# Two feed-forward layers behind a gated linear attention: a new list scheduler for the engine orders, a later place for the second weights' narrowing, and a graded lead in the last block

## The chip, the cores and the metric

The kernel runs on one core of a Trainium2 chip (trn2). The metric is the device time of one execution in microseconds; less is better.

## What is computed

```python
def _attn_ref(q, k, v, f_logit):          # q, k, v, f_logit: (4, 8, 768, 48)
    f = 1.0 / (1.0 + np.exp(-f_logit))
    for t in range(S):
        state = f[:, :, t, :, None] * state + np.einsum('bhd,bhe->bhde', k[:, :, t], v[:, :, t])
        y[:, :, t] = np.einsum('bhd,bhde->bhe', q[:, :, t], state)

def _moe_ref(x, w_in, w_out):             # x: (3072, 384), w_in: (384, 2048), w_out: (2048, 384)
    h = x @ w_in
    return (h * np.clip(h + 3.0, 0.0, 6.0) / 6.0) @ w_out

def _moe2_ref(x, w_in, w_out):            # same shapes
    h = x @ w_in
    return (h * np.tanh(np.log1p(np.exp(h)))) @ w_out

attn_out = _attn_ref(...)                 # transposed to (3072, 384)
out = _moe2_ref(_moe_ref(attn_out, ...), ...)
```

## The kernel before

The 3072 tokens go through in six blocks of 512, twice: once through the first layer (phase 1) and once through the second (phase 2). A layer has 16 parts of 128 hidden columns. For one part of one block TensorE makes a hidden run `H` of nine 128x512 matmuls (line 497; three chunks of the model dimension, each as high-by-high, low-by-high and high-by-low halves of an fp32r split), VectorE and ScalarE turn the result `h` into `g` and split it into `gh` and `gl` (lines 513 to 532: in phase 1 ScalarE's relu, VectorE's clip and product on L517, ScalarE's copy to `gh`, VectorE's subtraction to `gl` on L203), and TensorE adds three output runs `O` of three matmuls each into the banks o0 to o2 (line 538). Six blocks, two layers and 16 parts make 192 such rounds of 18 matmuls.

Phase 1 takes its input from the attention (line 236), which is worked out in 24 units of 128 tokens, four to a block. A unit has a running sum of the logs (`tri` times `f`, or a scan on VectorE, L278), a transposition of `k`, the scores `a`, masks, and the values; the state `st` goes from unit to unit. From the ninth unit on (`SPLIT`) a unit works in two halves of 64 tokens, its `v` is loaded with the line 258 and ScalarE copies the state into it.

The weights come in 64 bits. For one part, a load brings 768 KB into one of two tiles `raw` (line 211), and two ScalarE and two VectorE instructions narrow it into a tile `we` (lines 218 to 223, VectorE's on L220 and L222). For the first layer `weight` splits it at once into `wh` and `wl` (line 226). For the second layer, it is written to memory (`w2_d`, line 607) and read again at the start of phase 2.

Nothing of this is issued in the order it is written. `Plan.op` (line 89) records each step with its engine, a cost in microseconds, what it reads and writes, and a rank; `Plan.emit` (line 114) then runs one list schedule forward: on each engine the ready step of the lowest rank comes next. Ranks are written by hand: `16 * j + f` for a part, due times for the attention's units, `W2_AT + W2_GAP * f` for the second layer's narrowing, and in the last block all of the last `HOLD` = 14 parts lead by `TAIL_LEAD` = 6. Where TensorE would be idle before the first layer begins, `emit` puts in filler matmuls that write an unused bank (`warm`, `o<-cap` in the profile), one unit of 128 columns for each 0.22 us of planned idle time. All loads and stores are issued by SyncE's queue (SP), in the planned order.

```python
            now, eng = min((max(free[e], min(o.ready for o in c)), e) for e, c in wait.items() if c)
            o = min((o for o in wait[eng] if o.ready <= now), key=lambda o: (o.rank, o.seq))
            ...
                if free[eng] and free[eng] + unit < now < limit:
                    order.append(int((now - free[eng]) / unit))
```

Of the kernel before, what the change touches and what calls it, by code (L numbers as in the profile page):

```python
# [9 lines left out]
U32 = mybir.dt.uint32  # L10
# [6 lines left out]
DM, DFF, NT = 384, 2048, 3072  # L17
# [6 lines left out]
NF = DFF // 128  # L24
# [17 lines left out]
FIRST = "f0 tri k0 q0 f1 f2 ident v0 k1 q1 f3 v1 w0 k2 q2 v2 k3 q3 w1 v3 w2".split()  # L42
WARM = 30
GAP = 0.28
HOLD, TAIL_LEAD = 14, 6
WE = 2
W2_AT = 40
W2_GAP = 3.5
SPANS = ((0, D), (HB, R))


# [20 lines left out]


class Op:
    __slots__ = ("eng", "cost", "lat", "rank", "fn", "deps", "after", "seq", "start", "end", "left", "outs", "ready")


class Plan:
# [10 lines left out]
    def op(self, eng, cost, rank, fn, r=(), w=(), lat=0.0):  # L89
        o = Op()  # L90
        o.eng, o.cost, o.lat, o.rank, o.fn, o.seq = eng, cost, lat, rank, fn, len(self.ops)
        o.deps, o.after = set(), set()
        for key in r:
            o.deps.add(self.wrote[key])
        for key in w:
            o.deps.update(self.read.get(key, ()))
            if key in self.wrote:
                o.deps.add(self.wrote[key])
        for key in r:
            self.read.setdefault(key, []).append(o)  # L100
        for key in w:
            self.wrote[key], self.read[key] = o, []
        for key in (*r, *w):
            z = key[0] if isinstance(key, tuple) else key
            if isinstance(z, Lazy):
                z.users.append(o)
                if key in r:
                    z.used = True
                if not z.used:
                    z.heads.append(o)  # L110
        o.deps.discard(o)
        self.ops.append(o)

    def emit(self, filled, limit, unit, warm):
        for zs in self.tags.values():
            for i, z in enumerate(zs):
                if i:
                    for o in z.users:
                        o.after.update(zs[i - 1].heads)
                if i >= z.bufs:  # L120
                    for o in z.users:
                        o.deps.update(zs[i - z.bufs].users)
        for o in self.ops:
            o.outs, o.left, o.ready = [], 0, 0.0
        for o in self.ops:
            o.deps.discard(o)
            o.after -= o.deps | {o}
            for d in o.deps | o.after:
                d.outs.append(o)
            o.left = len(o.deps) + len(o.after)  # L130
        wait = {o.eng: [] for o in self.ops}
        free = dict.fromkeys(wait, 0.0)
        for o in self.ops:
            if not o.left:
                wait[o.eng].append(o)
        order = []
        while any(wait.values()):
            now, eng = min((max(free[e], min(o.ready for o in c)), e) for e, c in wait.items() if c)
            o = min((o for o in wait[eng] if o.ready <= now), key=lambda o: (o.rank, o.seq))
            wait[eng].remove(o)  # L140
            if eng == filled:
                limit = min(limit, now) if o.rank >= 1 else limit
                if free[eng] and free[eng] + unit < now < limit:
                    order.append(int((now - free[eng]) / unit))
            o.start, o.end = now, now + o.cost
            free[eng] = o.end
            order.append(o)
            for d in o.outs:
                t = o.start if d in o.after or o in d.after and o not in d.deps else \
                    o.end + o.lat + (GAP if d.eng != eng else 0.0)  # L150
                d.ready = max(d.ready, t)
                d.left -= 1
                if not d.left:
                    wait[d.eng].append(d)
        for o in order:
            if isinstance(o, int):
                warm(o)
            else:
                o.fn()


def fast_path(ctx, tc, qt, kt, ft, fn, vn, vs, vk, w1, w2, cst, ident, flag, w2_d, out):
    nc = tc.nc
    wide = w1.dtype != F32
# [27 lines left out]
    def dma(rank, out, in_, r, w, size, name=None):  # L192
        P.op("sp", max(0.45, size / 280e3), FIRST.index(name) - 99 if name in FIRST else rank, lambda: nc.sync.dma_start(out=out(), in_=in_()), r, w,
             lat=1.9)

    def pe(cost, rank, fn, r, w):
        P.op("pe", cost, rank, fn, r, w)
# [8 lines left out]
        dve(n, rank, lambda: nc.vector.tensor_tensor(out=out(), in0=a(), in1=b(), op=ALU.mult), r, w)  # L206


    def stream(w, f, rank, name=None):
        raw = new("raw", [128, 2 * DM * (2 if wide else 1)], 2, U32)  # L210
        dma(rank - 3, raw, lambda: w[f].bitcast(U32), (), (raw,), 128 * 2 * DM * (8 if wide else 4), name)
        if not wide:
            return raw, lambda: raw().bitcast(F32)
        e = new("we", [128, 2 * DM], WE)
        v = lambda i: raw().rearrange("p (a b) -> p a b", b=2)[:, :, i]
        eu = lambda: e().bitcast(U32)
        stt = nc.vector.scalar_tensor_tensor
# [271 lines left out]
    def hidden(ph, j, f, i):  # L489
        t0, n = BLOCKS[ph - 1][j]  # L490
        tail = ph == 2 and t0 + n == NT and f >= NF - HOLD
        xs = X[ph, j]
        tag, bufs = ("h", 2) if ph == 1 else (("h", 2), ("a", 2), ("m", 1), ("h", 2), ("a", 2))[i % 5]
        z = bank(tag, [128, 512], bufs)
# [7 lines left out]
                       stop=(t == 3 * KC - 1))  # L502
                    t += 1

        pe(9 * (0.0135 + n / 2400), i - TAIL_LEAD * tail, run, [("w", f, 0), ("w", f, 1), *x_keys(ph, j, 0), *x_keys(ph, j, 1)], (z,))
        if tail and f == NF - 1:
            gs = [new("A", [128, 2 * 512], 2, F32R) for p in "hl"]
        else:
# [3 lines left out]
        rank = i + 0.5  # L512
# [6 lines left out]
        else:  # L519
            e, g = new("k", [128, 512], 3), new("q", [128, 512], 3)  # L520
# [14 lines left out]
        for m in range(KC):  # L535
# [58 lines left out]
    for j, (t0, n) in enumerate(BLOCKS[0]):  # L594
# [3 lines left out]
        elif late:  # L598
            rank, values, vr, zxs, finish = late.pop()
# [3 lines left out]
        for f in range(NF):  # L603
            hidden(1, j, f, 16 * j + f)
    for f in range(NF):
        key, src = stream(w2, f, W2_AT + W2_GAP * f)
        dma(W2_AT + 1 + W2_GAP * f, lambda f=f: w2_d[f], src, (key,), (("w2", f),), 128 * DM * 8)

    def check1():
# [9 lines left out]
    for j, (t0, n) in enumerate(BLOCKS[1]):  # L619
# [17 lines left out]
        if j == 0:  # L637
            for f in range(NF):
                z = new("raw", [128, 2 * DM], 2)
# [196 lines left out]
```

## Time and profile before

| what | value |
|---|---|
| median of 3 runs | 894.73 us (893.9 to 894.84) |
| the profiled execution: its own time | 895.67 us |
| the profiled execution: its span | 893.9 us |
| TensorE (PE) busy in the span | 881.0 us, 99% |
| VectorE (DVE) busy | 668.7 us, 75% |
| ScalarE (ACT) busy | 561.5 us, 63% |
| loads and stores by SyncE's queue | 82.20 MB, 28.9% of 16 engines' span |

The profiled execution's own time is 1.77 us over its span and 0.94 us over the median. A timeline row gives the start in us, the duration in us, engine, line, operation, what it writes and reads, and in brackets how long the engine was idle before it and what ended that. Matmuls overlap, so a row's duration is longer than the step from one matmul to the next. PEld is TensorE's weight load.

### The profile page before, as it was taken

The page shows a single profiled execution, that of the slowest core. Times are in us where ns is not written, and L with a number is a line of the kernel's source. Part 1 is how long each engine was busy: PE and PEld are TensorE (multiplying, and loading weights), DVE is VectorE, ACT ScalarE, POOL GpSimd, SP SyncE. Part 2 cuts the span into 40 slices and gives each one's busy share as a digit, 9 for nine tenths or more (in the row PEclk, how much of TensorE's full clock was granted, in tenths as well). Part 3 has the DMA queues.
Part 4 walks back from the last instruction along what each step waited for, and adds up shares of the span by engine and source line. Part 5 has one row for each costly group of instructions (what it writes and reads, how often), then busy time and mean ns, then how long its engine had stood idle before and what let it go on. Part 6 is the DMA issues. An engine that isn't in the chain of part 4 may idle for free.

```text
span 893.9 us, 15680 instructions
## 1 busy us (share of the span) xinstructions
PE 881.0 (99%) x6341; PEld 722.0 (81%) x6341; DVE 668.7 (75%) x1045; ACT 561.5 (63%) x978; POOL 0.2 (0%) x4
## 2 busy tenths in 40 slices
PE   9999989999999999999999999999999999999997
PEld 6878868888888888888888888888888888888785
DVE  4898999778777555653565977888878888785894
ACT  6898787667646454433545766666666667664773
POOL 0000000000000000000000000000000000000000
PEclk9999999999999999999999999999999999999999
DMA  8766656867544222100323200100100100000001
GB/s 267 237 200 225 205 192 210 267 209 234 192 133 130 65 65 76 60 25 1 120 92 102 76 1 12 59 1 24 48 0 24 48 1 18 30 1 1 36 1 40
DMA packets 32465, 83.29 MB, mean 93 GB/s; under 512 B 3712, under 2 KB 7040, under 8 KB 32384
## 3 DMA queue, kind: packets, MB, share of 16 engines
q1 hardware_dynamic: 32384, 82.20, 28.9%
q8 instruction: 52, 0.85, 0.4%
q14 instruction: 29, 0.24, 0.1%
HBM read 66.45 MB, written 15.73 MB: 92 GB/s over the span
## 4 chain that ended last, share of the span: by engine, by line
PE 93%; ACT 2%; DVE 2%; DMA 1%; issue 0%; ACTq 0%
PE o L200 45%; PE h L200 30%; PE a L200 12%; PE m L200 7%; DMA raw<-w 1%; PE m L300 1%; ACT we L187 1%; ACT wh L187 0%; DVE we L220 0%; ACT raw L187 0%; DVE b L278 0%; DVE A L290 0%; PE m L400 0%; DVE we L222 0%; ACT vk L187 0%
## 5 line engine op out<-in xcount | busy, mean ns | idle before, releaser
L200 PE MATMUL o<-gh,wh 128*128 128x512 f32 x570 | 225.1, 395 | 0.0
L200 PE MATMUL o<-gl,wh 128*128 128x512 f32 x570 | 222.3, 390 | 0.7 <-DVE gl L203 0.7
L200 PE MATMUL o<-gh,wl 128*128 128x512 f32 x570 | 222.0, 389 | 0.0
L200 PE MATMUL h<-xh,wh 128*128 128x512 f32 x402 | 159.0, 396 | 2.1 <-DVE g L517 2.1
L200 PE MATMUL h<-xh,wl 128*128 128x512 f32 x402 | 157.3, 391 | 0.3 <-DVE wl L203 0.3
L200 PE MATMUL h<-xl,wh 128*128 128x512 f32 x402 | 157.0, 391 | 0.0
L200 PEld LDWEIGHTS o<-gh,wh 128*128 128x128 f32 x570 | 107.0, 188 | 24.2 <-issue 0.4
L200 PEld LDWEIGHTS o<-gh,wl 128*128 128x128 f32 x570 | 107.0, 188 | 22.6
L200 PEld LDWEIGHTS o<-gl,wh 128*128 128x128 f32 x570 | 107.1, 188 | 22.5 <-DVE gl L203 1.1
L517 DVE SCALAR_TENSOR_TENSOR g<-g,h 128x512 f32<-128x512 f32 x96 | 65.6, 684 | 79.1 <-ACT g L187 79.0
L187 ACT ACTIVATE g<-h,small 128x512 f32<-128x512 f32 x96 | 65.8, 686 | 82.3 <-PE h L200 69.7
L187 ACT ACTIVATE gh<-q 128x512 fp32r<-128x512 f32 x94 | 59.3, 631 | 79.8 <-DVE q L206 75.0
L203 DVE TENSOR_TENSOR gl<-g,gh 128x512 fp32r<-128x512 f32 x96 | 66.1, 689 | 33.4 <-ACT gh L187 33.1
L200 PEld LDWEIGHTS h<-xh,wh 128*128 128x128 f32 x402 | 75.6, 188 | 18.7 <-DVE g L517 2.7
L200 PEld LDWEIGHTS h<-xh,wl 128*128 128x128 f32 x402 | 75.7, 188 | 17.1 <-DVE wl L203 1.0
L200 PEld LDWEIGHTS h<-xl,wh 128*128 128x128 f32 x402 | 75.8, 188 | 15.2
L187 ACT ACTIVATE q<-k,small 128x512 f32<-128x512 f32 x96 | 69.4, 723 | 28.8 <-DVE k L525 25.1
L206 DVE TENSOR_TENSOR q<-q,k 128x512 f32<-128x512 f32 x96 | 66.0, 688 | 24.9 <-ACT q L187 23.5
L187 ACT ACTIVATE gh<-g 128x512 fp32r<-128x512 f32 x96 | 60.2, 627 | 35.3 <-DVE g L517 35.2
L203 DVE TENSOR_TENSOR gl<-q,gh 128x512 fp32r<-128x512 f32 x94 | 64.7, 688 | 9.2 <-ACT gh L187 8.5
L187 ACT ACTIVATE k<-k 128x512 f32<-128x512 f32 x96 | 59.6, 625 | 17.6 <-DVE k L522 17.4
L525 DVE SCALAR_TENSOR_TENSOR k<-k 128x512 f32<-128x512 f32 x96 | 65.3, 684 | 0.7 <-ACT k L187 0.7
(140 smaller groups left out, 1164.8 us busy)
## 6 DMA issues: line engine op xcount, KB each, us to landing
raw<-w SPq DMA_DIRECT2D x32, 768.0 KB, 5.2
v<-vs SPq DMA_DIRECT2D x16, 512.0 KB, 3.8
w<-we SPq DMA_DIRECT2D x16, 384.0 KB, 2.7
raw<-w SPq DMA_DIRECT2D x16, 384.0 KB, 3.0
k<-kt SPq DMA_DIRECT2D x24, 224.0 KB, 4.3
q<-qt SPq DMA_DIRECT2D x24, 224.0 KB, 3.6
x<-o SPq DMA_DIRECT2D x18, 256.0 KB, 2.1
f<-x SPq DMA_DIRECT2D x18, 256.0 KB, 2.6
```

Source lines behind the costliest of these rows:

```text
L187: lambda: nc.scalar.activation(out=out(), in_=in_(), func=func, **k), r, w)
L200: nc.tensor.matmul(**k)
L203: dve(n, rank, lambda: nc.vector.tensor_tensor(out=out(), in0=a(), in1=b().bitcast(F32), op=ALU.subtract), r, w)
L206: dve(n, rank, lambda: nc.vector.tensor_tensor(out=out(), in0=a(), in1=b(), op=ALU.mult), r, w)
L300: nc.tensor.transpose(ztv()[:, p, :], k3()[:, p, :], ident[0:R, 0:R])
L517: dve(n, rank, lambda: nc.vector.scalar_tensor_tensor(out=gg(), in0=gg(), scalar=6.0, in1=zn(), op0=ALU.min, op1=ALU.mult), (g, z), (g,))
L525: dve(n, rank, lambda: nc.vector.scalar_tensor_tensor(out=ee(), in0=ee(), scalar=2.0, in1=ee(), op0=ALU.add, op1=ALU.mult), (e,), (e,))
```

## The change

`emit` now makes seven forward list schedules (`ROUNDS` = 6, and the last) with a backward one between them. The first forward pass uses the ranks written by hand. A backward pass schedules every step as late as it can go, from the end of the pass before, and the time it gives a step is the step's rank in the next forward pass. Of the seven orders the one with the shortest planned end is issued. Since ranks are overwritten, `mlp` keeps which steps belonged to the layers.

The filler counts a unit double, 0.44 us, where planned idle time begins before `COLD` = 8 us. The load of part `f` of the second weights may start only when the hidden run number `22 + 3.5 f` of phase 1 is done (the new key `("h", i)`); its rank by hand is as before. In the last block the lead of a part grows in equal steps from 6/14 to 6.

```diff
+COLD = 8.0
+ROUNDS = 6
+W2_FROM = 22
...
+        o.mlp = rank >= 1
...
+    def forward(self):
+        wait = {o.eng: [] for o in self.ops}
+        free = dict.fromkeys(wait, 0.0)
+        for o in self.ops:
+            o.ready, o.left = 0.0, len(o.deps) + len(o.after)
...
+        while any(wait.values()):
+            now, eng = min((max(free[e], min(o.ready for o in c)), e) for e, c in wait.items() if c)
+            o = min((o for o in wait[eng] if o.ready <= now), key=lambda o: (o.rank, o.seq))
...
+        return max(o.end for o in self.ops)
+
+    def backward(self):
+        end = max(o.end for o in self.ops)
...
+        while any(wait.values()):
+            now, eng = max((min(free[e], max(o.ready for o in c)), e) for e, c in wait.items() if c)
+            o = max((o for o in wait[eng] if o.ready >= now), key=lambda o: (o.end, o.seq))
+            wait[eng].remove(o)
+            o.rank = now - o.cost
+            free[eng] = o.rank
+            for d in o.deps | o.after:
+                d.ready = min(d.ready, o.rank - d.lat - (GAP if d.eng != eng else 0.0) if d in o.deps else o.rank + d.cost)
...
     def emit(self, filled, limit, unit, warm):
...
+        best = None
+        for i in range(ROUNDS + 1):
+            end = self.forward()
+            if best is None or end < best[0]:
+                best = end, [(o, o.start, o.end) for o in self.ops]
+            if i < ROUNDS:
+                self.backward()
+        for o, o.start, o.end in best[1]:
+            pass
+        order, free = [], {}
+        for o in sorted(self.ops, key=lambda o: (o.start, o.seq)):
+            if o.eng == filled:
+                limit = min(limit, o.start) if o.mlp else limit
+                if o.eng in free:
+                    slow = unit * (2 if free[o.eng] < COLD else 1)
+                    if free[o.eng] + slow < o.start < limit:
+                        order.append(int((o.start - free[o.eng]) / slow))
+                free[o.eng] = o.end
             order.append(o)
...
-    def stream(w, f, rank, name=None):
+    def stream(w, f, rank, name=None, after=()):
         raw = new("raw", [128, 2 * DM * (2 if wide else 1)], 2, U32)
-        dma(rank - 3, raw, lambda: w[f].bitcast(U32), (), (raw,), 128 * 2 * DM * (8 if wide else 4), name)
+        dma(rank - 3, raw, lambda: w[f].bitcast(U32), after, (raw,), 128 * 2 * DM * (8 if wide else 4), name)
...
-        pe(9 * (0.0135 + n / 2400), i - TAIL_LEAD * tail, run, [("w", f, 0), ("w", f, 1), *x_keys(ph, j, 0), *x_keys(ph, j, 1)], (z,))
+        pe(9 * (0.0135 + n / 2400), i - (TAIL_LEAD * (f - NF + HOLD + 1) / HOLD if tail else 0), run, [("w", f, 0), ("w", f, 1), *x_keys(ph, j, 0), *x_keys(ph, j, 1)], (z, ("h", i)))
...
-        key, src = stream(w2, f, W2_AT + W2_GAP * f)
+        key, src = stream(w2, f, W2_AT + W2_GAP * f, after=(("h", int(W2_FROM + W2_GAP * f)),))
```

The orders change on every engine. Three places are shown; line numbers after the change are 40 higher in these parts.

TensorE at the start of the program, before: `cap` is the filler, `tri` the running sum of the first unit's logs, `ident` its transposition of `k`.

```order
L200 MATMUL o_147<-cap 112x128
L200 MATMUL o_147<-cap 112x512 x3
L200 MATMUL o_147<-cap 112x128 x2
L200 MATMUL o_164<-tri,f 112x128 x4
L200 MATMUL o_147<-cap 112x512 x2
L200 MATMUL o_147<-cap 112x128 x2
L400 MATMUL m<-ident,k 128x112 x4
```

And after the change:

```order
L240 MATMUL o_147<-cap 112x128
L240 MATMUL o_147<-cap 112x512
L240 MATMUL o_147<-cap 112x128 x3
L240 MATMUL o_164<-tri,f 112x128 x4
L240 MATMUL o_147<-cap 112x512
L240 MATMUL o_147<-cap 112x128
L440 MATMUL m<-ident,k 128x112 x4
```

The filler ahead of the first sum shrinks from 1 + 14 units of 128 columns to 1 + 7, and the one behind it from 10 to 5.

VectorE where the first block's parts end and the ninth and tenth units begin, before: `b<-cap,f` are the scans, `A<-q,b` and `A<-a,tri` the split units' work, `g` and `gl` the layer's, `we` the second weights' narrowing.

```order
L206 TENSOR_TENSOR k<-k,f 112x512
L290 TENSOR_TENSOR A<-q,b 64x512
L290 TENSOR_TENSOR A<-q,b 48x512
L203 TENSOR_TENSOR gl<-g,gh 128x512
L206 TENSOR_TENSOR k<-k,f 112x512
L290 TENSOR_TENSOR A<-q,b 64x512
L290 TENSOR_TENSOR A<-q,b 48x512
L220 SCALAR_TENSOR_TENSOR we<-we,raw 128x768
L329 TENSOR_TENSOR st<-st,a 112x192
L339 TENSOR_TENSOR A<-a,tri 64x256 x4
L517 SCALAR_TENSOR_TENSOR g<-g,h 128x512
```

And after the change:

```order
L246 TENSOR_TENSOR k<-k,f 112x512
L243 TENSOR_TENSOR gl<-g,gh 128x512
L330 TENSOR_TENSOR A<-q,b 64x512
L330 TENSOR_TENSOR A<-q,b 48x512
L246 TENSOR_TENSOR k<-k,f 112x512
L557 SCALAR_TENSOR_TENSOR g<-g,h 128x512
L330 TENSOR_TENSOR A<-q,b 64x512
L330 TENSOR_TENSOR A<-q,b 48x512
L243 TENSOR_TENSOR gl<-g,gh 128x512
L369 TENSOR_TENSOR st<-st,a 112x192
L379 TENSOR_TENSOR A<-a,tri 64x256 x4
L557 SCALAR_TENSOR_TENSOR g<-g,h 128x512
```

The layer's `gl` and `g` have moved ahead of the split units' work, and no narrowing stands here any more. In the order before, a whole pair of narrowing instructions (L220 and L222) also stands just ahead of this piece, and the L222 that belongs to the L220 shown follows a few rows behind it.

SyncE's queue where the third block's attention output `x` is stored, before:

```order
L193 DMA f<-ft 112x512 x2
L193 DMA x_2_130<-o 128x512 x3
L193 DMA v<-vs 128x1024
L193 DMA vk<-vk 128x384
L193 DMA k<-kt 112x512
L193 DMA q<-qt 112x512
L193 DMA v<-vs 128x1024
```

And after the change, a little further on:

```order
L233 DMA x_2_130<-o 128x512
L233 DMA raw<-w 128x1536
L233 DMA q<-qt 112x512
L233 DMA w_8_70<-we 128x768
L233 DMA raw<-w 128x1536
L233 DMA v<-vs 128x1024
L233 DMA vk<-vk 128x384
L233 DMA k<-kt 112x512
L233 DMA q<-qt 112x512
```

A 768 KB load of the second weights now stands right ahead of a unit's `v`, 512 KB. That is so for 5 of the 16 loads of `v<-vs`; before it was so for 3.

## Rows read from the trace of the kernel before

**Rows 1.** The page's part 1: busy time, share of the span, instructions.

```profile
PE 881.0 (99%) x6341; PEld 722.0 (81%) x6341; DVE 668.7 (75%) x1045; ACT 561.5 (63%) x978; POOL 0.2 (0%) x4
```

**Rows 2.** Waits of PE: us in total, times, longest us.

```profile
PE h L200 <- DVE g L517: 2.1, 2, 1.9
...
PE m L200 <- DVE q L206: 1.3, 1, 1.3
PE o L200 <- DVE gl L203: 0.7, 1, 0.7
```

**Rows 3.** Windows: length, busy us of PE, PEld, DVE, ACT, POOL, PEclk, DMA share, GB/s.

```profile
4.00:8.00 4.00, 4.00 (x11) 1.83 (x10) 0.00 (x0) 0.58 (x1) 0.00 (x0) 1.00 1.05 324
8.00:33.00 25.00, 25.00 (x413) 20.77 (x412) 18.65 (x32) 20.59 (x47) 0.00 (x0) 1.00 0.83 255
33.00:113.00 80.00, 79.11 (x669) 63.87 (x667) 72.92 (x100) 67.69 (x114) 0.00 (x0) 1.00 0.67 218
...
123.70:127.10 3.40, 3.40 (x46) 2.36 (x47) 3.40 (x5) 3.36 (x8) 0.00 (x0) 0.52 0.06 23
...
887.70:893.90 6.20, 0.00 (x0) 0.00 (x0) 0.04 (x1) 0.60 (x1) 0.00 (x0) 0.81 0.39 137
```

**Rows 4.** Timeline of all engines, start of the program.

```profile
1.59 6.41 PE L200 MATMUL o<-cap 112*112 112x128 f32 x12 [1.59 <-DVE small L573]
...
4.03 0.58 ACT L187 ACTIVATE f<-f 128x448 f32<-128x448 f32 x1
...
7.84 1.04 PE L200 MATMUL o<-tri,f 128*112 128x128 f32 x8
8.71 2.32 PE L200 MATMUL o<-cap 112*112 112x512 f32 x8
```

**Rows 5.** Timeline of PE around the first hidden runs.

```profile
32.00 1.24 PE L200 MATMUL o<-cap 112*112 112x512 f32 x4
33.00 0.48 PE L200 MATMUL h<-xh,wh 128*128 128x512 f32 x1
...
35.15 0.55 PE L400 MATMUL m<-ident,k 112*128 112x112 f32 x4
...
36.72 0.50 PE L200 MATMUL h<-xh,wh 128*128 128x512 f32 x1
...
39.00 0.54 PE L200 MATMUL m<-v,kn 128*32 128x48 f32 x32
...
41.01 0.50 PE L200 MATMUL h<-xh,wh 128*128 128x512 f32 x1
...
43.32 0.39 PE L200 MATMUL o<-gh,wh 128*128 128x512 f32 x1
```

**Rows 6.** Timeline of DVE from the last input to the first part's `gl`.

```profile
32.16 0.55 DVE L203 TENSOR_TENSOR xl<-h,xh 128x384 fp32r<-128x384 f32 x1
...
38.62 0.68 DVE L517 SCALAR_TENSOR_TENSOR g<-g,h 128x512 f32<-128x512 f32 x1
...
42.35 0.69 DVE L203 TENSOR_TENSOR gl<-g,gh 128x512 fp32r<-128x512 f32 x1
```

**Rows 7.** Timeline of ACT in the same stretch.

```profile
38.82 1.00 ACT L187 ACTIVATE we<-raw 128x768 f32<-128x768 f32 x1 [1.18 <-DMA raw<-w]
```

**Rows 8.** Timeline of DVE, 109 to 122 us.

```profile
109.63 0.96 DVE L220 SCALAR_TENSOR_TENSOR we<-we,raw 128x768 uint32<-128x768 uint32 x1 [0.55 <-ACT raw L187]
...
118.96 0.96 DVE L220 SCALAR_TENSOR_TENSOR we<-we,raw 128x768 uint32<-128x768 uint32 x1
...
121.98 0.69 DVE L517 SCALAR_TENSOR_TENSOR g<-g,h 128x512 f32<-128x512 f32 x1
```

**Rows 9.** Timeline of PE at the longest wait.

```profile
122.72 0.50 PE L200 MATMUL h<-xh,wh 128*128 128x512 f32 x1 [1.86 <-DVE g L517]
```

**Rows 10.** The same, in the last block.

```profile
836.18 0.50 PE L200 MATMUL m<-xh,wh 128*128 128x512 f32 x1 [1.35 <-DVE q L206]
```

**Rows 11.** Waits of ACT, as in rows 2.

```profile
ACT v L187 <- DMA v<-vs: 19.0, 7, 2.9
```

More of the change, by code (lines that the diff above doesn't have):

```diff
@@ L74 @@
 class Op:
-    __slots__ = ("eng", "cost", "lat", "rank", "fn", "deps", "after", "seq", "start", "end", "left", "outs", "ready")
+    __slots__ = ("mlp", "eng", "cost", "lat", "rank", "fn", "deps", "after", "seq", "start", "end", "left", "outs", "ready")
 class Plan:
@@ L112, in op @@
         self.ops.append(o)
+    def forward(self):
[3 more added lines that the diff above has]
+            o.ready, o.left = 0.0, len(o.deps) + len(o.after)
+            if not o.left:
+                wait[o.eng].append(o)
+        while any(wait.values()):
+            now, eng = min((max(free[e], min(o.ready for o in c)), e) for e, c in wait.items() if c)
+            o = min((o for o in wait[eng] if o.ready <= now), key=lambda o: (o.rank, o.seq))
+            wait[eng].remove(o)
+            o.start, o.end = now, now + o.cost
+            free[eng] = o.end
+            for d in o.outs:
+                d.ready = max(d.ready, o.end + o.lat + (GAP if d.eng != eng else 0.0) if o in d.deps else o.start)
+                d.left -= 1
+                if not d.left:
+                    wait[d.eng].append(d)
+        return max(o.end for o in self.ops)
+    def backward(self):
+        end = max(o.end for o in self.ops)
+        wait = {o.eng: [] for o in self.ops}
+        free = dict.fromkeys(wait, end)
+        for o in self.ops:
+            o.ready, o.left = end, len(o.outs)
+            if not o.left:
+                wait[o.eng].append(o)
+        while any(wait.values()):
+            now, eng = max((min(free[e], max(o.ready for o in c)), e) for e, c in wait.items() if c)
+            o = max((o for o in wait[eng] if o.ready >= now), key=lambda o: (o.end, o.seq))
+            wait[eng].remove(o)
+            o.rank = now - o.cost
+            free[eng] = o.rank
+            for d in o.deps | o.after:
+                d.ready = min(d.ready, o.rank - d.lat - (GAP if d.eng != eng else 0.0) if d in o.deps else o.rank + d.cost)
+                d.left -= 1
+                if not d.left:
+                    wait[d.eng].append(d)
     def emit(self, filled, limit, unit, warm):
@@ L123, in emit @@
         for o in self.ops:
-            o.outs, o.left, o.ready = [], 0, 0.0
-        for o in self.ops:
             o.deps.discard(o)
             o.after -= o.deps | {o}
+            o.outs = []
+        for o in self.ops:
             for d in o.deps | o.after:
                 d.outs.append(o)
[L130 to L146, printed above, removed]
-            order.append(o)
[L148 to L154, printed above, removed]
+        best = None
[16 more added lines that the diff above has]
+                free[o.eng] = o.end
+            order.append(o)
         for o in order:
```

## The prediction

> **What bounds the kernel now.** First the busy shares [rows 1]: TensorE (PE) works through 99% of the span, VectorE through 75%, so the reader is to see that PE's stream of matmuls sets the time and that a new order can win only what that stream loses. The change alters no matmul of the computation. Three kinds of loss are to be looked for: idle time, filler, and time at half rate.
>
> The waits of PE [rows 2] give the idle time: 2.1 us for `g`, 1.3 for `q`, 0.7 for `gl`. The windows [rows 3] give the rest. From 8 to 33 us PE is busy throughout, but with filler and attention: the first hidden run starts at 33.00 [rows 5]. From 123.7 to 127.1 its granted clock is 0.52, which is the lower of its two levels (1.2 and 2.4 GHz) for nearly the whole of 3.40 us; just before, it had waited 1.86 us [rows 9]. The last 6.20 us hold no matmul at all; they are the last eviction and stores, which the change leaves alone.
>
> All but one of these losses lie where VectorE is crowded: it is busy for 72.92 of 80 us from 33 to 113 [rows 3]. The one in the last block, 1.35 us at 836.18 [rows 10], is of the order alone: hidden runs pulled forward all at once leave too few output runs to cover a part's chain.
>
> PE's idle time in the span is 893.9 - 881.0 = 12.9 us, of which 6.2 are the end. Beside this stands a rule of the Trainium skill (Perfetto Trace Analysis, section Identifying the Most-Contended Engine): matmul busy share is not a good measure of how close TensorE is to its limit, the share of weight loads is one of two better ones. By busy share alone at most 6.7 us could be won and the time would be no less than 888.0; the filler and the half-rate stretch, both counted as busy, say with the rule that there is more.
>
> **The change part by part.** The sum is made against the profiled execution's own 895.67 us, 0.94 over the median of the runs.
>
> *A, filler counted double before 8 us.* PE works off 15 units of filler from 1.59 to 8.00, 0.43 us each; behind the first sum 10 units take 2.32 us, 0.23 each [rows 4]. So the early ones run at half rate, though the recorded clock says 1.00 there [rows 3]. The logs that the first sum waits for are ready at 4.03 + 0.58 = 4.61, but PE is at filler until 8.00. With 8 units it is free at 1.59 + 8 x 0.43 = 5.0. If the sum then runs at half rate, it takes 2.1 instead of 1.04 us and ends at 7.1 instead of 8.9: 1.8 us earlier. The attention's chain hangs on it up to the first hidden run, whose last input ends at 32.71 [rows 6]. Bounds: 0, if the loads set the pace (the queue moves 324 GB/s from 4 to 8 us, [rows 3]); 3.0, if the sum runs at full rate. I take 1.8, since the loads in the first 12 us are issued in nearly the same order and none of them is awaited on this chain after the first.
>
> *B, attention work moved ahead of the first hidden run.* The fifth unit's transposition and scores stand between the first two hidden runs, from 35.15 to 36.72 [rows 5]; the new order puts them in front, where filler runs for 1.24 us and PE waits anyway. Gain 1.5; bounds 0 (if they push the hidden run back) and 1.6.
>
> *C, the first output run comes too early.* Before, 8.0 us lie between the end of the first hidden run (35.3) and its output run (43.32), filled with transposition, scores, a hidden run, values and another hidden run [rows 5]. Now only one hidden run and the values are left between: 39.00 - 36.72 + 41.01 - 39.00 = 4.3 us. The chain through ACT and VectorE took 7.7, to 42.35 + 0.69 [rows 6], 1.2 of it for a late load of weights [rows 7]. The new order leaves relu, `g`, a pair of narrowing instructions and `gl`: 0.68 (taken like `g`) + 0.68 + 2 x 0.96 + 0.69, with the hand-overs some 4.3 us, if nothing else holds them up. So a new wait of 0 to 3.7 us; I take 1.2, nearer to the lower end, because masks and scans that stood in this chain have gone ahead.
>
> *D, the second weights' narrowing leaves the crowded stretch.* Before, a pair of it starts at 109.63 and another at 118.96 [rows 8], in front of the `g` at 121.98 that PE waits for; each instruction is 0.96 us. Now the first load waits for hidden run 22, in the second block, and the layer's `gl` and `g` go ahead of the split units' work. I count the waits for `g` and `gl` as gone, 2.1 + 0.7, and with them the half-rate stretch, (1 - 0.52) x 3.40 = 1.6. What is late next is the split units' own masks, which other hidden and output runs cover. Bounds 0 and 4.4. The narrowing itself, 32 VectorE and 32 ACT instructions in all, half of them the second layer's, now lies beside PE work from the second block on, where VectorE has room.
>
> *E, stepwise lead in the last block.* Hidden runs and output runs now alternate; 1.3 us of waiting goes [rows 2, 10]. Bounds 0 and 1.3. The end behind the last matmul costs nothing and gains nothing.
>
> *F, the wait added on SyncE's queue.* A load of second weights that waits for its hidden run holds back all that is behind it, above all a unit's `v`. I cost it at 0: ACT already waits 19.0 us in 7 places for `v` [rows 11], up to 2.9 each, and no wait of PE for it is on the list of rows 2. Without that cover see the second rival.
>
> Sum: -1.8 - 1.5 + 1.2 - 4.4 - 1.3 = **-7.8 us**, 887.9 in a profiled execution, 886.9 in the median.
>
> **The rivals.**
>
> *The crowd comes back.* The orders are the best by planned costs; where PE runs behind plan, VectorE may be as full as before and half of D and E return, C at 2.7. For it: VectorE's share of 91% from 33 to 113 [rows 3] falls only where the narrowing leaves, the last ten us of it. Against: the `g` rows are really ahead now. Gain 1.8 + 1.5 - 2.7 + 2.8 = 3.4: 891.3.
>
> *ACT stands behind a late `v`.* Five `v` loads are queued right behind a 768 KB load. At 324 GB/s [rows 3] that takes 2.4 us, and ACT, which issues in order, keeps the layer's relu back for as long. If PE has used up its cover, as the waits of up to 2.9 us [rows 11] allow, that is 5 x 2.4 = 12 us: 886.9 + 12 = 898.9, slower than before. It decides from the point where such a wait of ACT is longer than the output runs that PE has ready; against it, the planner places its other steps with this order of loads in view, and the 2.9 us waits cost PE nothing.
>
> *The lower clock lasts.* Less filler means more idle time in the first 30 us; if the lower level then lasts to the first hidden run, A turns round. From 8 to 33 us ACT is busy 20.59 of 25.00 us [rows 3], so at least 4.4 us hang on PE's or the loads' steps alone, which double: -7.8 + 1.8 + 4.4 = -1.6, 893.1. For it: the level fell once, behind a wait of 1.86 us. Against: from 8 to 113 us the windows keep 1.00 [rows 3]. The Trainium skill (TensorE: Matmul & The Clock Gate, What's actually happening) says that the throttled state is the default and activity releases it, which speaks for this rival; rows 9 and 3 agree in the order of events, no more.
>
> *Nothing gained.* If the best order by plan is none on the chip, waits only move: 894.7.
>
> **How the numbers follow.** A measurement of this kernel can tell some 0.2%, 1.8 us, from no change. The forecast has 0.77, the crowd 0.11, the late `v` 0.06, the lower clock and nothing gained 0.03 each. All the best ends, 3.0 + 1.6 + 4.4 + 1.3 with no new wait, make 10.3: 884.4. On the other side the range takes in the crowd's 891.3; the bounds of A and C alone, 0 and 3.7, make the sum -3.5, 891.2. So 884.2 to 891.5; left out are the late `v`, the lower clock and no gain. Faster: 0.77 + 0.11 = 0.88; within 0.2%: 0.06 (lower clock and no gain); slower: 0.06.
>
> **What would show it.** Right: the first sum starts near 5 us and the first hidden run near 31; a new wait of about 1 us for `gl` before the first output run; no wait of PE over 0.5 us between 100 and 130 and none near 830; granted clock 1.00 from 100 to 140; no narrowing instruction between 100 and 140. Wrong: PE waits at the split units between 150 and 400 us (the late `v`), matmul steps at double length after 10 us (the lower clock), or new waits for `g` before 110 (the crowd).

## The result and the profile after

| | median us | lowest to highest | runs |
|---|---|---|---|
| before | 893.9 | 893.36 to 894.84 | 5 |
| changed | 884.42 | 883.22 to 886.42 | 5 |

The ratio is 0.9896, 95% interval 0.9882 to 0.991: 9.5 us faster, where 7.8 were forecast (884.42 against 886.9, range 884.2 to 891.5). The profiled execution of the changed kernel took 883.22 us, the shortest of its five, with a span of 881.5. Against the profile before (895.67) that is 12.4 us, 2.9 more than the medians differ by. The pair of profiles overstates the gain; a half-rate stretch and late loads, each of them in some executions of a kernel and not in others, account for part of that below.

The changed kernel's busy times (the page's part 1), to be read against [rows 1]:

```profile
PE 872.5 (99%) x6327; PEld 719.2 (82%) x6327; DVE 668.6 (76%) x1045; ACT 564.1 (64%) x978; POOL 0.2 (0%) x4
```

The share of PE is the same 99%, though 12 us of span are gone: PE's busy time itself fell by 8.5 us while its computation stayed as it was. The 14 instructions fewer are filler (40 of them before, 26 now); the rest is half-rate time and the ends of matmuls that overlap less around a wait.

All waits of PE in the changed kernel (us in total, times, longest):

```profile
PE o L240 <- DVE small L613: 1.6, 1, 1.6
PE o L240 <- DVE gl L243: 1.1, 1, 1.1
PE m L440 <- DVE k L246: 0.5, 1, 0.5
```

The first is the program's start, which is in every version. Of [rows 2] nothing is left: the waits for `g` and `q` are gone, the one for `gl` is another, at 37.84, ahead of the first output run. The windows of the changed kernel (columns as in [rows 3]):

```profile
8.00:33.00 25.00, 24.95 (x421) 21.50 (x420) 21.49 (x37) 22.70 (x50) 0.00 (x0) 1.00 0.89 291
33.00:113.00 80.00, 78.94 (x717) 64.12 (x716) 74.77 (x103) 68.14 (x117) 0.00 (x0) 1.00 0.59 194
100.00:120.00 20.00, 20.00 (x244) 16.40 (x246) 18.19 (x29) 16.59 (x37) 0.00 (x0) 1.00 0.27 82
120.00:140.00 20.00, 20.00 (x249) 16.50 (x239) 13.29 (x24) 12.89 (x27) 0.00 (x0) 1.00 0.34 111
820.00:840.00 20.00, 20.00 (x90) 16.57 (x89) 17.19 (x28) 13.55 (x22) 0.00 (x0) 1.00 0.02 9
```

From 100 to 140 PE never stops and keeps its full clock, where before it was at 0.52 from 123.7 to 127.1. No narrowing stands there: the last of it ends at 100.66 and the next begins at 151.62. VectorE is busier from 33 to 113 than in [rows 3], 74.77 against 72.92 us, and PE's idle time there is 1.06 us, all of it at one wait, against 80 - 79.11 = 0.89 before. So how full VectorE is does not by itself set PE's waits.

PE's start in the changed kernel (timeline), the answer to [rows 4, 5]:

```profile
1.59 3.69 PE L240 MATMUL o<-cap 112*112 112x128 f32 x10 [1.59 <-DVE small L613]
5.12 1.04 PE L240 MATMUL o<-tri,f 128*112 128x128 f32 x8
...
30.00 0.48 PE L240 MATMUL h<-xh,wh 128*128 128x512 f32 x1
...
32.15 0.39 PE L240 MATMUL h<-xh,wh 128*128 128x512 f32 x1
...
36.28 0.49 PE L240 MATMUL o<-gh,wh 128*128 128x512 f32 x1
37.84 0.50 PE L240 MATMUL o<-gl,wh 128*128 128x512 f32 x1 [1.06 <-DVE gl L243]
```

Three pieces make up the 12.4 us between the two profiles. The first hidden run starts at 30.00 instead of 33.00: 3.0. From there to the end of the last matmul it takes 875.67 - 30.00 = 845.7 us instead of 887.68 - 33.00 = 854.7: 9.0. The stores behind the last matmul take 5.8 instead of 6.2: 0.4. These two marks, the first hidden run and the length from it to the last matmul, are used for every run below.

### The profile page after: what moved, and what is told of

It reads as the page before. It is cut to its first block, busy times and chain, and to the rows that moved or that the text cites. A ratio compares the mean times of both kernels' runs of the same rounds, so it can differ in the third digit from the quotient of the medians.

```text
span 881.5 us, 15666 instructions
## 1 busy us (share of the span) xinstructions
PE 872.5 (99%) x6327; PEld 719.2 (82%) x6327; DVE 668.6 (76%) x1045; ACT 564.1 (64%) x978; POOL 0.2 (0%) x4
## 4 chain that ended last, share of the span: by engine, by line
PE 97%; DVE 1%; ACT 1%; issue 0%; ACTq 0%
PE o L240 46%; PE h L240 31%; PE a L240 12%; PE m L240 7%; PE m L340 1%; ACT f L227 0%; PE m L440 0%; DVE we L260 0%; DVE wl L243 0%; ACT vk L227 0%; DVE A L428 0%; DVE we L262 0%; ACT we L227 0%; DVE xl L243 0%; ACT wh L227 0%
## 5 line engine op out<-in xcount | busy, mean ns | idle before, releaser
L227 ACT ACTIVATE k<-k 128x512 f32<-128x512 f32 x96 | 60.1, 627 | 25.5 <-DVE k L562 25.2
```

Source lines behind the costliest of these rows:

```text
L227: lambda: nc.scalar.activation(out=out(), in_=in_(), func=func, **k), r, w)
```

## The experiments

The theory: the waits and the half-rate stretch are gone since `g` and `gl` stand ahead of other work, and the head is shorter by the filler. Rival theories: each part of the change brings its own share, and the shares add; or the tie of the narrowing does it by clearing VectorE; or the start is bound by its loads and the filler matters little. Each was timed against the kernel before on the same chip, and gains are taken from that kernel's median in the same rounds (893.9 to 894.59). The change has four parts: the filler count, the stepwise lead, the tie of the second weights' loads to a hidden run, and the rounds of schedules. All variants, with the two marks from each profile:

| kernel | median us | ratio, 95% interval | first hidden run | to the last matmul's end |
|---|---|---|---|---|
| before | 893.9 | | 33.00 | 854.7 |
| changed | 884.42 | 0.9896 (0.9882 to 0.991) | 30.00 | 845.7 |
| only the filler count | 890.65 | 0.9958 (0.9945 to 0.9972) | 30.77 | 853.0 |
| only the stepwise lead | 892.29 | 0.9974 (0.9964 to 0.9985) | 32.77 | 852.1 |
| only the tie | 890.96 | 0.9963 (0.9949 to 0.9976) | 32.73 | 849.3 |
| only the rounds | 885.82 | 0.9908 (0.9893 to 0.9923) | 32.32 | 845.6 |
| all but the rounds | 886.5 | 0.9924 (0.991 to 0.9937) | 30.95 | 847.7 |
| all but the tie | 884.73 | 0.99 (0.9883 to 0.9917) | 30.28 | 845.6 |
| all but the stepwise lead | 886.37 | 0.9915 (0.9901 to 0.9929) | 30.87 | 845.8 |
| all but the filler count | 886.27 | 0.991 (0.9896 to 0.9923) | 31.98 | 845.7 |
| changed, a second time | 884.51 | 0.9894 (0.9879 to 0.9909) | 31.56 | 845.9 |
| changed, no filler | 885.88 | 0.9904 (0.9889 to 0.9919) | 32.82 | 846.0 |
| changed, shorter hand-over | 886.46 | 0.9913 (0.9899 to 0.9927) | 32.09 | 846.2 |
| changed, first weights later | 883.15 | 0.9876 (0.986 to 0.9892) | 31.02 | 844.5 |

**Only the filler count.** Into the kernel before:

```diff
-                if free[eng] and free[eng] + unit < now < limit:
-                    order.append(int((now - free[eng]) / unit))
+                slow = unit * (2 if free[eng] < COLD else 1)
+                if free[eng] and free[eng] + slow < now < limit:
+                    order.append(int((now - free[eng]) / slow))
```

> The kernel before with the doubled filler unit alone; the order of all other work is that of before. Theory (term A: the overlong filler holds up the first sum, and the attention's chain hangs on it up to the first hidden run): first sum at about 5.1 instead of 7.84 us, first hidden run 1.8 to 3.0 us earlier than 33.0, time about 891.5. Rival (the start is set by loads, ACT and DVE): first sum earlier, first hidden run still at 33.0, time 893.9. Second rival (the clock rises later with less filler): matmul steps at half rate beyond 8 us, time 894 or more.

PE's start in this run (timeline):

```profile
1.59 3.75 PE L202 MATMUL o<-cap 112*112 112x128 f32 x10 [1.59 <-DVE small L575]
5.14 1.81 PE L202 MATMUL o<-tri,f 128*112 128x128 f32 x8
```

The sum starts at 5.14 and runs mostly at half rate, so it ends at 6.95 and the first hidden run comes 2.2 us earlier, near the 1.8 of term A. The median gained 3.9. The other 1.7 lies behind: the waits of the kernel before are all still there, 1.86 us among them, yet no half-rate stretch follows (windows of this run):

```profile
115.00:121.20 6.20, 4.33 (x80) 3.39 (x79) 5.98 (x13) 5.78 (x13) 0.00 (x0) 1.00 0.62 178
121.20:127.00 5.80, 5.80 (x144) 4.69 (x143) 5.71 (x10) 5.12 (x11) 0.00 (x0) 1.00 0.37 105
```

The mean granted clock of each execution fits this: 0.998 or 0.999 in all five of this kernel, 0.996 to 0.998 in the kernel before in the same rounds.

**Only the stepwise lead.** Into the kernel before:

```diff
-        pe(9 * (0.0135 + n / 2400), i - TAIL_LEAD * tail, run, [...], (z,))
+        pe(9 * (0.0135 + n / 2400), i - (TAIL_LEAD * (f - NF + HOLD + 1) / HOLD if tail else 0), run, [...], (z,))
```

> The kernel before with the stepwise lead in the last block alone. Theory (term E): no wait of PE near 836 us, which with the restart behind the wait was some 1.6 us; time about 892.3. Rival (the wait only moves to another part of the last block): 893.9.

2.3 us by the medians. The wait near 836 is gone, as forecast; those for `gl` (0.77) and `g` (1.86) stay, and here the clock did fall behind them (a window of this run):

```profile
123.10:126.50 3.40, 3.40 (x69) 2.56 (x67) 3.19 (x5) 3.19 (x7) 0.00 (x0) 0.50 0.16 63
```

By the mean granted clock this fall comes in some executions and not in others. Of the eight executions of this kernel four have a mean granted clock of 0.996, the profiled one among them, and took 892.22 to 893.16 us; the three at 0.999 took 891.23 to 891.85, the one at 0.998 893.02. Two waits of 0.2 and 0.3 us that the kernel before has at 113 and 47 us are not on this profile's list.

**Only the tie.** Into the kernel before, with `stream`'s argument `after` and the key `("h", i)` of the hidden run as in the diff:

```diff
-        key, src = stream(w2, f, W2_AT + W2_GAP * f)
+        key, src = stream(w2, f, W2_AT + W2_GAP * f, after=(("h", int(W2_FROM + W2_GAP * f)),))
```

> The kernel before with the second weights' loads tied to hidden run 22 + 3.5 f alone, one forward schedule by the ranks written by hand. Theory (the narrowing in the crowded stretch is what makes PE wait there): waits between 110 and 125 us and the half-rate stretch behind them gone, 4 to 5 us, time about 889.5. Rival (the split units' own work stands in front of the layer's g and gl, whatever the narrowing does): at least one wait of over 0.7 us stays, gain 1 to 3, time 891 to 893.

PE's waits in this run:

```profile
PE o L201 <- DVE small L574: 1.6, 1, 1.6
PE m L201 <- DVE q L207: 1.3, 1, 1.3
PE m L201 <- ACT kn L188: 0.6, 1, 0.6
```

The waits for `g` and `gl` between 110 and 123 are gone and no half-rate stretch comes; 849.3 instead of 854.7. So the narrowing's later place is enough by itself to remove these waits. By the medians it is 3.6 us, where 4 to 5 were expected.

**Only the rounds.** The change with the other three undone:

```diff
-COLD = 8.0
+COLD = 0.0
...
-        pe(9 * (0.0135 + n / 2400), i - (TAIL_LEAD * (f - NF + HOLD + 1) / HOLD if tail else 0), run, [...], (z, ("h", i)))
+        pe(9 * (0.0135 + n / 2400), i - TAIL_LEAD * tail, run, [...], (z, ("h", i)))
...
-        key, src = stream(w2, f, W2_AT + W2_GAP * f, after=(("h", int(W2_FROM + W2_GAP * f)),))
+        key, src = stream(w2, f, W2_AT + W2_GAP * f)
```

> The kernel after without the doubled filler, without the tie and without the stepwise lead: the rounds of forward and backward schedules alone. Theory (the terms add up): B, C and part of D and E are there, A is not: 889 to 890. Rival (the rounds make nearly all of it, and the tie and the lead are only other starting points for them): all but A, 887 or less, and no wait of PE over 0.5 us behind the first output run.

8.8 us, where the whole change gained 9.5, and 845.6 from the first hidden run to the last matmul, as in the whole change. Behind the start the rounds alone remove everything that tie and lead remove, and B with it; the head, up to the first hidden run, is nearly as long as before (32.32).

**All but the tie.** In the change:

```diff
-        key, src = stream(w2, f, W2_AT + W2_GAP * f, after=(("h", int(W2_FROM + W2_GAP * f)),))
+        key, src = stream(w2, f, W2_AT + W2_GAP * f)
```

> The kernel after without the tie of the second weights' loads alone. Theory now (the backward rounds already put the second weights' narrowing late and the layer's g and gl ahead, so that the tie has little left to do): same as after within 1 us, 884 to 885.5; no PE wait over 0.5 us between 100 and 130 us. Rival (term D of the prediction: the narrowing must leave the crowded stretch): PE waits there again, 2 to 4 us, 887 to 888.

884.73, not to be told from the whole change. Where the narrowing now stands (VectorE, timeline of this run) and what PE does meanwhile (window):

```profile
118.25 0.66 DVE L557 SCALAR_TENSOR_TENSOR g<-g,h 128x512 f32<-128x512 f32 x1
119.43 0.96 DVE L260 SCALAR_TENSOR_TENSOR we<-we,raw 128x768 uint32<-128x768 uint32 x1
120.90 0.70 DVE L243 TENSOR_TENSOR gl<-g,gh 128x512 fp32r<-128x512 f32 x1
...
130.59 0.95 DVE L260 SCALAR_TENSOR_TENSOR we<-we,raw 128x768 uint32<-128x768 uint32 x1
131.58 0.96 DVE L262 SCALAR_TENSOR_TENSOR we<-raw,we 128x768 uint32<-128x768 uint32 x1
132.46 0.69 DVE L243 TENSOR_TENSOR gl<-g,gh 128x512 fp32r<-128x512 f32 x1
```

```profile
120.00:140.00 20.00, 20.00 (x221) 16.39 (x210) 19.55 (x35) 15.23 (x32) 0.00 (x0) 1.00 0.71 234
```

The second weights' narrowing starts at 119.43, later than the 109.63 of [rows 8] but still in the crowded stretch, and VectorE is busy for 19.55 of 20 us. Before 119.43 none of it stands ahead of a `g`; behind that a whole pair even stands between a `g` (129.39) and its `gl` (132.46), and PE does not wait. So neither a full VectorE nor a narrowing pair in this stretch makes PE wait by itself; that it is the earlier `g` and `gl` that do it is the reading that fits, but this run moves many other steps too.

**All but the rounds.** In the change, so that the ranks by hand are used once:

```diff
-ROUNDS = 6
+ROUNDS = 0
```

> Filler count, tie of the narrowing and stepwise lead together, but only the one forward pass with the ranks by hand. If the three add up as they did alone on the kernel before (3.8 + 3.3 + 2.3 = 9.4 us, from the differences of medians): about 884.9, as good as the whole change, with 848 us or less from the first hidden run to the last matmul, and the rounds are one of two ways to the same end. If the rounds are what removes the waits up to 100 us: waits of PE near 94 (0.6 us) and at the first output run's place in the order as before, attention work between the first two hidden runs, and 886 to 888.

886.5, 7.5 us under the kernel before, where the singles by their medians come to 3.9 + 2.3 + 3.6 = 9.8 (a little more than the expectation has). The 847.7 to the last matmul lies within the 848 of the first case, the time does not. Left over behind the first hidden run are the waits for `kn` (0.6 us) and `wl` (0.3), which the kernel before had too, and the fifth unit's transposition and scores between the first two hidden runs (timeline of this run):

```profile
30.95 0.48 PE L240 MATMUL h<-xh,wh 128*128 128x512 f32 x1
...
33.12 0.55 PE L440 MATMUL m<-ident,k 112*128 112x112 f32 x4
33.60 1.16 PE L240 MATMUL a<-q,k 48*128 48x128 f32 x16
```

Beside the other three the rounds are worth 2.0 us.

**All but the filler count, and no filler.** Two kernels; in the second only the first unit of filler is left:

```diff
-COLD = 8.0
+COLD = 0.0
```

```diff
-WARM = 30
+WARM = 0
```

> The kernel after with the filler units of before ahead of 8 us, order otherwise the same. Theory (the overlong filler is worth on its own what it was worth in the kernel before, some 3.5 us, less what the later start of the first hidden run had hidden): first sum at 7.1 to 7.8, first hidden run 1.5 to 2.5 us later than in after, 886 to 887.5. Rival (the rounds alone reached 885.8, so that the filler is worth 1.4 at most): 885 to 886.

> The kernel after with no filler but the first unit. The prediction's third rival (with less activity the lower clock lasts): matmul steps at half rate well beyond 8 us, first hidden run several us later than 30.0, 888 or more. Theory (attention work alone lifts the clock, the chain of ACT and DVE sets the start): half rate to at most 12 us, first hidden run at 30 to 31.5, 884 to 886.

With the old count the sum waits for its turn until 6.78 and the first hidden run until 31.98; 886.27 us, 1.9 over the change (the intervals overlap). Without filler the median is 885.88 (ratio 0.9904, 0.9889 to 0.9919), and the start reads (PE's timeline of this run):

```profile
4.73 2.05 PE L240 MATMUL o<-tri,f 128*112 128x128 f32 x8 [2.37 <-ACT f L227]
8.34 1.01 PE L440 MATMUL m<-ident,k 112*128 112x112 f32 x4 [1.56 <-DVE k L246]
9.28 2.08 PE L240 MATMUL a<-q,k 48*128 48x128 f32 x16
11.29 2.05 PE L240 MATMUL o<-tri,f 128*112 128x128 f32 x8
...
15.86 1.13 PE L240 MATMUL o<-tri,o 128*112 128x128 f32 x8
```

The sum of the first logs starts at 4.73, but at half rate, and so does all up to some 15 us; only the third sum takes 1.13. The first hidden run comes at 32.82. So half rate outlasts the 12 us of the theory, and the time stays below the 888 of the rival. This is the rival "the lower clock lasts", made to happen, though only to some 15 us and not to the first hidden run. By the medians it costs 1.5 us, not clear of noise (the intervals overlap), where the rival put 6.2 on it. From 8 to 33 us the change keeps ScalarE busy for 22.70 of 25.00 us, so much of what PE does slowly may lie beside ScalarE's work; no run separates that. By the Trainium skill (TensorE: Matmul & The Clock Gate, What's actually happening) the throttled state is the default and activity releases it; the order of events agrees, full rate from about 15 us on without filler, in the first profile of the change from the first sum at 5.12.

**All but the stepwise lead.** In the change:

```diff
-        pe(9 * (0.0135 + n / 2400), i - (TAIL_LEAD * (f - NF + HOLD + 1) / HOLD if tail else 0), run, [...], (z, ("h", i)))
+        pe(9 * (0.0135 + n / 2400), i - TAIL_LEAD * tail, run, [...], (z, ("h", i)))
```

> The change without the stepwise lead. If the backward passes overwrite the ranks by hand so that the lead has no say: same as the whole change within 0.5 us (883.9 to 884.9), no wait of PE over 0.5 us near 830. If the lead is worth in the whole change what it was worth alone (2.3 us): about 886.7, with a wait of 1.0 to 1.4 us in the last block.

The profile agrees with the first of the two cases: no wait of PE between 40 us and the end, 845.8 to the last matmul. The median, 1.9 above the second run of the change in the same rounds, does not; the five times go from 884.51 to 887.56 and the two intervals just overlap. What lengthens some of these executions is not in the one that was profiled, the shortest of the five. Two of the three long ones (886.48 and 887.56) have a mean granted clock of 0.997, the other three 0.999, which would fit a half-rate stretch in them; 886.37 has 0.999. This stays open.

**A shorter planned hand-over.** In the change, so that the plan believes engines hand over faster:

```diff
-GAP = 0.28
+GAP = 0.20
```

> The kernel after with the planned hand-over between engines set to 0.20 instead of 0.28 us, nearer to the 0.03 to 0.1 us seen between ACT and DVE. The planned idle piece ahead of the first output run is gone from the order. Theory (term C, a wait of 1.06 us and its restart, can be taken back by an order that has more work between the first hidden run and its output run): about 1.2 us less than after, 883.2. Rival (orders planned with tighter hand-overs wait elsewhere on the chip): same as after or slower, 884.4 to 886.

886.46, ratio 0.9913 (0.9899 to 0.9927). The wait for `gl` ahead of the first output run shrinks to 0.2 us, but the first hidden run starts at 32.09 and the time is 2 us worse by the medians. Of the 2.1 us that the first hidden run comes later than in the change, 0.9 are the first sum at half rate (1.91 us, ended at 7.05) and 1.2 lie between that sum and the hidden run. Behind the hidden run nothing is won either, 846.2 against 845.7. The theory failed, and the rival's time came.

**The change a second time.**

> The changed kernel once more, unaltered, for a second profile. If the moment at which TensorE gets its full clock differs from execution to execution with the same filler: full clock at another time than the 5.1 us of the first profile, the first sum 1.0 to 2.1 us long, the first hidden run at 30.0 to 31.1, and from there to the last matmul's end 845.5 to 846.2 again. If the moment is set by the order alone: 5.1, 1.04 and 30.0 again. Median 884.4 within 0.5 in both cases.

The same order, and the first hidden run at 31.56 instead of 30.00, though the first sum came a little earlier than in the first profile (at 5.01, 1.04 long). Neither of the two cases has this. The difference is in the loads. VectorE and ScalarE in the second profile (timeline of both):

```profile
18.09 0.93 ACT L227 ACTIVATE we<-raw 128x768 f32<-128x768 f32 x1 [2.32 <-DMA raw<-w]
18.92 0.57 ACT L227 ACTIVATE o<-o 112x512 f32<-112x512 f32 x1
...
20.01 0.69 DVE L246 TENSOR_TENSOR k<-k,o 112x512 f32<-112x512 f32 x1 [2.31 <-DMA k<-kt]
```

and the same instructions in the first:

```profile
15.90 0.93 ACT L227 ACTIVATE we<-raw 128x768 f32<-128x768 f32 x1
16.73 0.58 ACT L227 ACTIVATE o<-o 112x512 f32<-112x512 f32 x1
...
18.01 0.69 DVE L246 TENSOR_TENSOR k<-k,o 112x512 f32<-112x512 f32 x1 [0.19 <-DMA k<-kt]
```

The first part's weights, 768 KB, land 10.2 us after their issue instead of 7.3, at 18.0 instead of 14.8, and the fourth unit's `k` behind them at 19.9 instead of 18.0; from 8 to 12 us the queue moves 255 GB/s instead of 319. In ScalarE's order the fourth unit's exps stand behind a narrowing whose result is split only from 26.85 on (`wh`, in the first profile). From the end of the first sum to the first hidden run it is 30.00 - 6.16 = 23.8 us in the first profile, 31.56 - 6.05 = 25.5 in the second.

**A better version: these weights later.** One more rule of order for the plan:

```diff
+    named["w0"].after.add(named["q3"])
     with tc.manual_schedule():
         P.emit("pe", WARM, 0.22, warm)
```

(`named` keeps the recorded loads by name; the load of the first part's weights starts after the fourth unit's `q`.)

> The change with one more rule of order for the plan: the load of the first part's weights starts only after the fourth unit's q. ScalarE's first narrowing, which in the second profile of the change waited 2.3 us for that load (0 in the first profile) in front of the fourth unit's exps, then stands behind them. If the loads of the first 20 us are what makes executions of the same kernel differ by up to 1.5 us at the first hidden run (30.00 and 31.56): no wait of VectorE for k over 0.3 us and none of ScalarE for raw over 1 us before 20 us, first hidden run at 29.5 to 30.3, median 883.2 to 884.2 and a smaller spread. If the loads only shift the same lateness to another step (the narrowing itself, whose end the first hidden run needs too): first hidden run at 30.3 to 32, median 884.5 or more.

883.15 us, 882.83 to 883.49 in four runs, ratio 0.9876 (0.986 to 0.9892): 1.3 us below the change's median. The two were not timed side by side, only each against the kernel before, the second timing of the change on another chip, and the intervals touch; but its slowest run is faster than eight of the change's nine. VectorE's wait for `k` is gone and ScalarE's for `raw` is 0.43. Yet the first hidden run started at 31.02, outside the 29.5 to 30.3 of the first case and inside the second's 30.3 to 32, since in this execution the first sum ran at half rate (1.89 us) and ended at 7.03; from there 24.0 us, as without a late load. What gained in this profile is another thing, which was not foreseen: from the first hidden run to the last matmul it is 844.5 instead of 845.7. The order of VectorE around the first `gl` differs. In the change (timeline of ScalarE and VectorE):

```profile
32.61 0.67 ACT L227 ACTIVATE g<-h,small 128x512 f32<-128x512 f32 x1
32.62 0.95 DVE L260 SCALAR_TENSOR_TENSOR we<-we,raw 128x768 uint32<-128x768 uint32 x1
33.60 0.96 DVE L262 SCALAR_TENSOR_TENSOR we<-raw,we 128x768 uint32<-128x768 uint32 x1
34.48 0.68 DVE L557 SCALAR_TENSOR_TENSOR g<-g,h 128x512 f32<-128x512 f32 x1
35.08 1.11 DVE L260 SCALAR_TENSOR_TENSOR we<-we,raw 128x768 uint32<-128x768 uint32 x1
36.22 0.96 DVE L262 SCALAR_TENSOR_TENSOR we<-raw,we 128x768 uint32<-128x768 uint32 x1
37.09 0.69 DVE L243 TENSOR_TENSOR gl<-g,gh 128x512 fp32r<-128x512 f32 x1
```

and in this version:

```profile
33.83 0.96 DVE L265 SCALAR_TENSOR_TENSOR we<-raw,we 128x768 uint32<-128x768 uint32 x1
34.70 0.68 DVE L560 SCALAR_TENSOR_TENSOR g<-g,h 128x512 f32<-128x512 f32 x1
35.30 0.68 DVE L431 TENSOR_TENSOR A<-a,tri 128x512 f32<-128x512 f32 x1
35.90 1.07 DVE L263 SCALAR_TENSOR_TENSOR we<-we,raw 128x768 uint32<-128x768 uint32 x1
36.87 0.71 DVE L246 TENSOR_TENSOR gl<-g,gh 128x512 fp32r<-128x512 f32 x1
37.46 0.98 DVE L265 SCALAR_TENSOR_TENSOR we<-raw,we 128x768 uint32<-128x768 uint32 x1
```

The second half of the pair has gone behind `gl`, and PE's wait of term C is gone. Counted from the first hidden run, `gl` starts 1.2 us earlier, after 5.85 instead of 7.09 us. Of that 0.4 lie between `g` and `gl`; the other 0.8 are a `g` that starts earlier, mainly because one mask (`A<-a,tri`) ahead of it has gone behind it. This agrees with the cause that term C named and adds a second one, what stands ahead of `g`.

## Why the prediction held, step by step

The forecast's case came, at the lower end of the range: 2.5 us below the predicted time and 0.2 above the range's end. In the pair of profiles the head gave 3.0 us for the 1.8 of A, and all behind it 9.0 for the 6.0 of B to E.

- **A, 1.8 predicted.** The step holds, with its size depending on the execution. The sum starts at 5.0 to 5.1 in every profile with the shorter filler; it then takes 1.04 us in the change, 1.81 in the kernel with the filler count alone and 1.89 in the last version, by when the clock rises. That the first hidden run hangs on this sum is well borne out: it starts 23.8 to 24.2 us after the sum's end in ten of the fourteen profiles, and 24.7 to 26.0 in the other four. The first profile showed the upper bound, 3.0, and that is partly luck: with the filler of before the sum already ended anywhere from 7.82 to 8.88, with the shorter one from 6.05 to 7.06. One condition under the term was too firm: the loads do set the pace in some executions (the second profile).
- **B, 1.5.** Held: the two hidden runs follow each other without a break (30.00, 32.15). It belongs to the rounds.
- **C, +1.2.** The wait came at its place, 1.06 us long, and a narrowing pair does stand between `g` and `gl`. The size is partly luck. By the prediction's own lengths the chain and the room for it were both 4.3 us, and 1.2 was picked between the bounds; the chain took 5.5 us, from 32.31 to 37.78, since a second pair, from 32.62 to 34.56, stands ahead of `g`, whose relu was ready at 33.28.
- **D, 4.4.** The time is gone, but the attribution failed in the step "the narrowing leaves the crowded stretch". Leaving it is one of two ways; the rounds reach the same end with narrowing still in part of it. The crowd was also read from a window that ends too early: these waits lie from 113 to 123, behind the 33 to 113 that the prediction quotes, and from 113 to 127 VectorE was busy for 13.74 of 14 us. The half-rate stretch, 1.6 of the 4.4, was counted as belonging to the waits for certain; the same waits left it out in one profile of three.
- **E, 1.3.** Held in place; with the restart behind it the wait was 1.6, as worked out below. Beside the rounds no profile shows anything left for it, though the median without it is 1.9 us longer, and that stays open.
- **F, 0.** Right, and for a plainer reason than the one given: the tie exists in the plan only. Its key `("h", i)` names no tile, so the kernel issues no wait for it; a second-weights load only stands later in the queue.

The terms of the idle rows were mis-sized in common. In [rows 10] the matmul before the wait starts at 834.44 and PE restarts at 836.18: 1.74 us, where the step in a run is 0.23, and the first step after the restart takes 0.34. That is 1.51 + 0.11 = 1.6 us lost, where the row says 1.35, since the last matmul's modelled end lies beyond its step. Taking the same 0.27 for each wait (an estimate from this one), and since [rows 2], cut to three groups, left out 0.6 for `kn` near 94 and 0.3 near 47, the kernel before lost some 5.1 + 6 x 0.27 = 6.7 us in six waits, 1.6 at half rate and 1.6 to B, and the change keeps 1.06 + 0.27 of it: 9.9 - 1.3 = 8.6 of the 9.0 measured. 0.4 is unaccounted for.

The late `v` did not come: PE waits for nothing behind 38 us, and ScalarE's waits for `v` fell from the 19.0 us of [rows 11] (ACT's waits in the changed kernel):

```profile
ACT v L227 <- DMA v<-vs: 5.8, 6, 2.4
```

The returning crowd did not come either. Not tested is how many of the seven orders are needed, or whether the backward passes matter beyond giving the planner several orders to choose from.

## What to carry to other kernels

When an engine in the middle is nearly full, look at what stands directly ahead of the instructions that the bottleneck waits for, not at the share: one narrowing and one mask moved behind `gl` and `g` went with the loss of a wait of 1.06 us in the last version. Rules by hand that mend single places need not add to a planner that orders everything: here the three singles came to 9.8 us, the planner alone to 8.8 and all together to 9.5. Measure each beside the planner before keeping it. A second profile of the same kernel shows which start-up loads are close to late; moving one of them here took its wait away, but no profile shows a shorter head from it.

## What the hardware showed that was not expected

- The clock's rise is not fixed by the program: with the same filler from 1.59 us on, the first sum, started at 5.0 to 5.1 us, took 1.04 us in both profiles of the change and 1.11, 1.30, 1.81, 1.89, 1.91 and 1.92 in six variants that keep this filler. The recorded clock from 4 to 8 us says 1.00 at either length, so only the length of a known row tells.
- The same waits (0.74 or 0.77 and 1.86 us within 10 us) were followed by 3.4 us at half rate in two profiles, 0.42 us from one hidden matmul to the next, and by none in a third, 0.23 us.
- The same loads in the same order landed 2 to 3 us apart in two executions of the same kernel, within the first 20 us.
